# A windowed attention with a two-layer MLP: 128 bytes more behind the tile of queries and keys

## The chip, the cores and the metric

One core of a Trainium2 chip runs the program. The metric is the device time in microseconds (us). "Faster" and "slower" always mean the kernel after the change against the kernel before.

## The reference, cut to what matters

Inputs are `q`, `k`, `v` of shape (8, 8, 576, 64), `moe_w_in` (512, 2048) and `moe_w_out` (2048, 512), all float32. What is computed:

```python
scores = np.matmul(q, k.transpose(0, 1, 3, 2)) / 8
mask_plain = (rel >= 0) & (rel < 32)                         # heads 0 to 3
mask_dil = (rel >= 0) & (rel < 128) & (rel % 4 == 0)         # heads 4 to 7
attn = softmax(where(mask, scores, -1e9))
x = (attn @ v), heads side by side, reshaped to (4608, 512)
h = x @ w_in
g = where(h >= 1, h, where(h <= -1, 0, (h + 1) ** 2 / 4))
out = g @ w_out                                              # (4608, 512)
```

## The kernel before, in words

The two matrix products of the MLP carry nearly all the work. Each of the 4608 tokens' rows belongs to one of nine token tiles of 512 (`t` = 0 to 8), and the 2048 hidden features to sixteen chunks of 128 (`f` = 0 to 15). Operands are split into a high and a low float32r part, and a product is the sum of three matmuls: high by high, high by low, low by high.

- **Layer 1** (`layer1`, the matmuls of line 504): for one (t, f) 12 matmuls (4 blocks of 128 input features, three terms each). The stationary operand is a 128x128 slice of the weight tile `wi`, the moving operand 512 columns of `xh` or `xl`. The result is the PSUM bank `h`.
- **Activation** (lines 514 to 536): VectorE clamps, ScalarE squares, VectorE takes the larger, ScalarE casts the high part `gh`, VectorE subtracts to get the low part `gl`.
- **Layer 2** (`layer2`, line 550): for one (t, f) 12 matmuls (4 blocks of 128 tokens, three terms each). The stationary operand is a 128x128 slice of `gh` or `gl`, the moving operand 512 columns of the weight tile `wo`. The results add up in four PSUM banks `acc` over all f.

I call the 12 matmuls of one layer at one (t, f) a group. There are 9 x 16 groups of each layer. Weight tile `wi0` holds the high and low part of f = 0 and 1, `wi1` of f = 2 and 3, and so on to `wi7` (f = 14 and 15); `wo0` to `wo7` likewise. `weight` (line 488) cuts the slices: one of 128 columns starts a multiple of 512 bytes behind the start of its tile.

The attention runs beside it, on pairs of heads (n = 0 to 31). Queries and keys of a pair, already transposed on the host, come by one DMA into one tile with the tag `qk` (`load_qk`, line 112; queries in columns 0 to 575, keys in columns 576 to 1183), and the values of two pairs into one tile with the tag `v` (`load_v`). In the loop over (t, f) a pair's values are multiplied and the scores of the next pair are made in a *visit* (`visit_step`, line 579; matmuls of line 383 and line 205) between layer 1 and layer 2 of every fourth step; 24 pairs are done so. The stationary slices of `v` follow each other at 256 bytes, the moving slices of `pts` at 384 bytes (line 383).

Order of work. For token tile 0 a list written out by hand (`FIRST`) gives the order on all five engines; it also holds the loads and the splitting of the weights (`raw`, `P`, `B`, `J`, `D`, `E`). The weight blocks are loaded in this order: wi0, wi1, wo0, wi2, wo1, wo3, wi6, wo4, wi3, wo2, wi4, wo7, wi7, wo6, wi5, wo5. For tiles 1 to 8 a loop writes the order of TensorE and of the SP queue (which issues the DMAs): layer 1 of step s, layer 2 of step s - 2, with the attention's pieces in fixed slots; the other engines are ordered by the scheduler. Step s is (t, f) = divmod(s, 16).

Where the tiles lie. A pool puts its tiles one behind the other in a partition, in the order in which their tags are first asked for, so a tile's address follows from the sizes of those ahead of it. In bytes of a partition:

| tiles, in order of address | first and last start | start modulo 256 | modulo 512 |
|---|---|---|---|
| small, pts | 1152, 3712 | 128 | 128 |
| wi6, wo6, wi7, wo7, three xh, three xl | 8320 to 82048 | 128 | 128 |
| two c | 90240, 93568 | 128 | 128, 384 |
| qk (4736 bytes) | 96896 | 128 | 128 |
| v | 101632 | 0 | 256 |
| wi0 to wi5, wo0 to wo5, three gh, three gl, y, m0, m1, mixed | 107776 to 220416 | 0 | 256 |

All sizes behind `qk` are multiples of 2048 bytes, and so are those of the wi, wo, xh and xl ahead of it. The last tile ends at byte 228608.

Of the kernel before, what the change touches and what calls it, by code (L numbers as in the profile page):

```python
# [6 lines left out]
F32 = mybir.dt.float32  # L7
# [7 lines left out]
B, H, S, D = 8, 8, 576, 64  # L15
# [4 lines left out]
KPAD = S + 32  # L20
# [44 lines left out]
def body(ctx, tc, qk, v, mask, mask4, w_in, w_out, out):  # L65
# [4 lines left out]
    pool = ctx.enter_context(tc.tile_pool(name="pool", bufs=1))  # L70
# [41 lines left out]
    def load_qk(n):  # L112
        hd = heads.setdefault(n, {})
        if "qk" not in hd:
            hd["qk"] = pool.tile([128, S + KPAD], F32, tag="qk", name=f"qk{n}")
        hd["q"], hd["k"] = hd["qk"][:, :S], hd["qk"][:, S:]
        nc.sync.dma_start(out=hd["qk"], in_=qk[n])

# [460 lines left out]
    def visit_step(s, n):  # L579
        o, sc = visit(s, n)  # L580
        joint_values(n, o)
        if n + 1 < NP:
            scores(n + 1, at=sc)
        if n + 2 < NP:
            load_qk(n + 2)
        if n + 1 < NP and n % 2:
            load_v(n + 1)
# [37 lines left out]
    def small_step(count):  # L625
        small_constants(int(count), banks_of((4, 5), "small")[1])

    STEPS = {
        "fill": filling_step, "small": small_step,
        "qk": pair(load_qk), "v": lambda n, q=None: load_v(int(n), QUEUES[q]),  # L630
        "raw": lambda _, name, q=None: fetch((name[:2], int(name[2:])), queue=QUEUES[q]),
        "S": lambda n: scores(int(n), BANKS.get("S" + n)),
# [135 lines left out]
```

## Time and profile before

| | us |
|---|---|
| median of 3 runs | 897.12 (896.67 to 897.38) |
| the profiled execution's own time | 897.7 |
| its span, first to last instruction | 895.9 |
| TensorE matmul busy | 885.3 (99%) |
| VectorE busy | 546.4 (61%) |
| ScalarE busy | 305.0 (34%) |
| GpSimd busy | 126.7 (14%) |

The 1.8 us between the profiled time and the span lie around the program's instructions. The profile's engines are PE (TensorE matmul), PEld (TensorE weight load, beside PE), DVE (VectorE), ACT (ScalarE), POOL (GpSimd), SP (the DMA queue). A matmul's record overlaps the next one's (a mean of 394 ns each), so the time of a group is read from where the next group starts, not from these durations.

### The profile page before, as it was taken

The numbers are of one execution on the slowest core, as the hardware profiler recorded it, in microseconds if no ns is written. First come the engines' busy times: TensorE is split into PE (matmuls) and PEld (weight loads), VectorE is DVE, ScalarE is ACT, GpSimd is POOL, SyncE is SP. The second block draws the span as 40 slices with busy tenths as digits, with TensorE's granted clock in tenths as the row PEclk, the third lists the DMA queues.
The fourth block names the chain that finished last, engine by engine and source line by source line (L and its number), as shares of the span: only waits on it lengthen the run. The fifth ranks groups of instructions, "written<-read, shape, count | busy, mean of one in ns | idle before, by whom it ended". The sixth has DMA issues, their size and how long they took to land.

```text
span 895.9 us, 15568 instructions
## 1 busy us (share of the span) xinstructions
PE 885.3 (99%) x6680; PEld 716.7 (80%) x6680; DVE 546.4 (61%) x888; ACT 305.0 (34%) x490; POOL 126.7 (14%) x80
## 2 busy tenths in 40 slices
PE   8899999999999999999999999999999999999998
PEld 7677778888888888888888888888888888888886
DVE  7888876566666666566666666566656543334332
ACT  3797543222323233323323232223322222222222
POOL 2455441111010111111111010111111000000000
PEclk9999999999999999999999999999999999999999
DMA  9971012101210021101210121002110010001001
GB/s 367 401 308 63 29 63 75 64 28 64 75 60 32 4 99 36 64 28 64 75 64 28 64 75 40 35 17 98 41 63 1 1 48 1 1 0 48 1 1 47
DMA packets 17172, 59.77 MB, mean 67 GB/s; under 512 B 1904, under 2 KB 2160, under 8 KB 15056
## 3 DMA queue, kind: packets, MB, share of 16 engines
q1 hardware_dynamic: 17104, 58.79, 17.8%
q8 instruction: 52, 0.85, 0.4%
q14 instruction: 16, 0.13, 0.0%
HBM read 49.34 MB, written 9.44 MB: 66 GB/s over the span
## 4 chain that ended last, share of the span: by engine, by line
PE 95%; DVE 4%; issue 0%; ACT 0%; POOL 0%; POOLq 0%
PE acc L550 44%; PE h L504 43%; PE os L383 3%; PE os L205 2%; PE s L205 1%; PE o L370 1%; DVE m_wo L475 1%; DVE m_wi L475 0%; DVE gl L536 0%; DVE c L273 0%; PE s L184 0%; PE fill L138 0%; PE s L223 0%; PE small L145 0%; DVE wo_first L341 0%
## 5 line engine op out<-in xcount | busy, mean ns | idle before, releaser
L550 PE MATMUL acc<-wo,gh 128*128 128x512 f32 x1152 | 383.7, 394 | 0.0
L504 PE MATMUL h<-xh,wi 128*128 128x512 f32 x1152 | 362.4, 394 | 0.2
L504 PEld LDWEIGHTS h<-xh,wi 128*128 128x128 f32 x1152 | 216.1, 188 | 51.0 <-DVE gl L536 1.0
L550 PEld LDWEIGHTS acc<-wo,gh 128*128 128x128 f32 x1152 | 216.4, 188 | 50.2 <-ACT gh L531 0.4
L550 PE MATMUL acc<-wo,gl 128*128 128x512 f32 x576 | 225.7, 392 | 1.4 <-DVE gl L536 1.4
L504 PE MATMUL h<-xl,wi 128*128 128x512 f32 x576 | 227.0, 394 | 0.0
L520 ACT ACTIVATE y<-y,small 128x512 f32<-128x512 f32 x144 | 104.1, 723 | 318.9 <-DVE y L514 318.9
L514 DVE TENSOR_SCALAR y<-h 128x512 f32<-128x512 f32 x144 | 99.2, 689 | 125.3 <-PE h L504 124.2
L524 DVE TENSOR_TENSOR h<-h,y 128x512 f32<-128x512 f32 x144 | 100.5, 698 | 99.4 <-ACT y L520 99.4
L536 DVE TENSOR_TENSOR gl<-h,gh 128x512 fp32r<-128x512 f32 x144 | 99.3, 690 | 55.1 <-ACT gh L531 53.5
L504 PEld LDWEIGHTS h<-xl,wi 128*128 128x128 f32 x576 | 108.1, 188 | 24.9 <-DVE xl L357 0.3
L550 PEld LDWEIGHTS acc<-wo,gl 128*128 128x128 f32 x576 | 108.3, 188 | 24.6 <-DVE gl L536 1.7
L531 ACT CAST gh<-h 128x512 fp32r<-128x512 f32 x144 | 84.5, 587 | 103.9 <-DVE h L524 101.7
L281 POOL TENSOR_TENSOR c<-c 96x768 f32<-96x768 f32 x28 | 41.2, 1472 | 439.2 <-DVE c L273 438.8
L317 DVE STREAM_TRANSPOSE pts<-c 32x384 f32<-32x384 f32 x168 | 95.3, 567 | 3.0 <-POOL c L303 0.6
L303 POOL TENSOR_TENSOR c<-c 96x768 f32<-96x768 f32 (+1 forms) x30 | 43.5, 1450 | 87.9 <-DVE c L299 87.9
L288 DVE TENSOR_REDUCE c<-c 96x12 f32<-96x768 f32 (+1 forms) x30 | 28.0, 933 | 38.8 <-ACT c L285 38.8
L285 ACT ACTIVATE c<-c 96x768 f32<-96x768 f32 (+1 forms) x30 | 25.0, 834 | 49.0 <-POOL c L281 38.7
L353 ACT CAST xh<-os 128x384 fp32r<-128x384 f32 (+7 forms) x48 | 19.2, 400 | 42.0 <-DVE c L249 21.9
L383 PEld LDWEIGHTS os<-pts,v 128*64 128x64 f32 x576 | 24.6, 137 | 8.8 <-DVE gl L536 6.6
L383 PE MATMUL os<-pts,v 128*64 128x96 f32 x576 | 29.1, 250 | 0.0
L205 PE MATMUL s<-qk 64*32 64x64 f32 x1188 | 27.0, 220 | 0.8 <-issue 0.8
(100 smaller groups left out, 389.9 us busy)
## 6 DMA issues: line engine op xcount, KB each, us to landing
qk<-qk_in SPq DMA_DIRECT2D x29, 592.0 KB, 3.9
v<-v_in SPq DMA_DIRECT2D x29, 384.0 KB, 4.7
raw_wi<-w_in SPq DMA_DIRECT2D x8, 1024.0 KB, 14.4
raw_wo<-w_in SPq DMA_DIRECT2D x8, 1024.0 KB, 15.4
out<-out SPq DMA_DIRECT2D x32, 256.0 KB, 2.0
wi_first<-qk_in SPq DMA_DIRECT2D x2, 592.0 KB, 6.8
out<-outs SPq DMA_DIRECT2D x4, 256.0 KB, 2.0
wo_first<-v_in SPq DMA_DIRECT2D x2, 384.0 KB, 9.3
```

The costliest lines, as they stand in the source:

```text
L205: PE.matmul(out=sps[j][QB * g : QB * g + QB, KW * t : KW * t + KW], lhsT=hd["q"][r, QB * b : QB * b + QB], rhs=hd["k"][r, QB * b : QB * b ...
L281: nc.gpsimd.tensor_tensor(out=c, in0=c, in1=spread(n, 0), op=ALU.subtract)
L303: engine.tensor_tensor(out=c, in0=c, in1=spread(n, 2), op=ALU.mult)
L317: nc.vector.transpose(out=pt[r : r + 32, :, 32 * g : 32 * g + 32], in_=c[32 * g : 32 * g + 32, :, 32 * h : 32 * h + 32],)
L383: PE.matmul(out=at[64 * j : 64 * j + 64, 96 * t : 96 * t + 96], lhsT=hd["v"][:, j, t], rhs=pts[:, j, t], start=True, stop=True,)
L504: PE.matmul(out=hp, lhsT=weight("wi", f, w, slice(128 * c, 128 * c + 128)), rhs=xtile(t)[x][:, c], start=start and (c, w, x) == terms[0], ...
L514: nc.vector.tensor_scalar(out=gs[t, f][0], in0=hps[t, f], scalar1=-1.0, scalar2=1.0, op0=ALU.max, op1=ALU.min)
L520: nc.scalar.activation(out=y, in_=y, func=AF.Square, bias=half_t, scale=0.5)
L524: done.append([nc.vector.tensor_tensor(out=hp, in0=hp, in1=gs[t, f][0], op=ALU.max)])
L531: done[-1].insert(0, nc.scalar.copy(out=g_tile("gh", t, f), in_=hps[t, f]))
L536: nc.vector.tensor_tensor(out=g_tile("gl", t, f), in0=hp, in1=gh.bitcast(F32), op=ALU.subtract)
L550: PE.matmul(out=acc[m], lhsT=g[:, 128 * m : 128 * m + 128], rhs=weight("wo", f, w, slice(0, DM)), start=f == 0 and i == 0, stop=f == NF - ...
```

## The change: what it does

The `qk` tile is asked for with 1216 columns instead of 1184, that is 4864 bytes instead of 4736, and the first 1184 columns are used as before. Nothing else differs: the same instructions with the same shapes, the same DMA of 592 KB per pair. The `qk` tile itself starts where it did. Every tile behind it (v, wi0 to wi5, wo0 to wo5, gh, gl, y, m0, m1) starts 128 bytes later: at 128 modulo 256, or 384 modulo 512.

```diff
@@ load_qk (line 112)
         if "qk" not in hd:
-            hd["qk"] = pool.tile([128, S + KPAD], F32, tag="qk", name=f"qk{n}")
+            hd["qk"] = pool.tile([128, 1216], F32, tag="qk", name=f"qk{n}")[:, :S + KPAD]
         hd["q"], hd["k"] = hd["qk"][:, :S], hd["qk"][:, S:]
```

## Rows read from the trace of the kernel before

**Rows 1.** The page: busy time by engine, and the chain that ended last.

```profile
span 895.9 us, 15568 instructions
PE 885.3 (99%) x6680; PEld 716.7 (80%) x6680; DVE 546.4 (61%) x888; ACT 305.0 (34%) x490; POOL 126.7 (14%) x80
...
PE 95%; DVE 4%; issue 0%; ACT 0%; POOL 0%; POOLq 0%
PE acc L550 44%; PE h L504 43%; PE os L383 3%; PE os L205 2%; PE s L205 1%; PE o L370 1%; DVE m_wo L475 1%; DVE m_wi L475 0%; DVE gl L536 0%; DVE c L273 0%; PE s L184 0%; PE fill L138 0%; PE s L223 0%; PE small L145 0%; DVE wo_first L341 0%
```

**Rows 2.** Busy time by stretch: us, each engine's busy time and count, clock, DMA.

```profile
125.60:321.00 195.40, 195.39 (x1538) 158.77 (x1539) 125.12 (x206) 58.48 (x100) 25.74 (x18) 1.00 0.15 53
321.00:700.00 379.00, 379.00 (x2941) 307.55 (x2942) 240.34 (x397) 113.61 (x193) 44.65 (x31) 1.00 0.14 49
700.00:789.70 89.70, 89.70 (x409) 73.36 (x410) 35.26 (x52) 22.62 (x36) 0.00 (x0) 1.00 0.03 12
```

**Rows 3.** The chain of waits, token tile 8: start us, us, what.

```profile
798.06 2.79 PE h L504 x12
...
803.64 2.78 PE h L504 x12
...
812.01 2.74 PE acc L550 x12
814.75 2.79 PE h L504 x12
817.54 2.73 PE acc L550 x12
...
858.96 2.79 PE h L504 x12
...
864.50 2.73 PE h L504 x12
...
872.69 2.73 PE acc L550 x12
875.42 2.73 PE h L504 x12
878.15 2.80 PE acc L550 x12
880.94 2.76 PE h L504 x12
883.70 8.38 PE acc L550 x36
```

**Rows 4.** The chain of waits where tile 1 passes into tile 2.

```profile
204.53 2.73 PE h L504 x12
207.26 2.73 PE acc L550 x12
...
220.49 2.79 PE acc L550 x12
223.28 2.79 PE h L504 x12
...
237.22 1.14 PE os L383 x24
```

**Rows 5.** Line 383: durations min/median/max ns, and what ended its engine's idle time (us, times).

```profile
L383 PE MATMUL os<-pts,v x576: 246/246/297, 139.8 to 700.9; 128*64 128x96 f32 x192
...
  DVE gl L536: 6.6, 18
```

**Rows 6.** Timeline ahead of one visit: start us, us, what.

```profile
480.04 0.69 DVE L536 TENSOR_TENSOR gl<-h,gh 128x512 fp32r<-128x512 f32 x1
...
480.84 0.28 PEld L383 LDWEIGHTS os<-pts,v 128*64 128x64 f32 x6 [0.37 <-DVE gl L536]
```

**Rows 7.** Token tile 0: busy time by stretch, columns as in rows 2.

```profile
28.00:60.00 32.00, 29.81 (x214) 22.81 (x210) 28.66 (x41) 26.97 (x39) 15.39 (x7) 1.00 0.99 409
60.00:100.00 40.00, 40.00 (x346) 32.26 (x346) 33.84 (x50) 30.05 (x41) 23.49 (x11) 1.00 0.16 52
100.00:125.60 25.60, 25.45 (x262) 19.58 (x260) 22.28 (x31) 15.17 (x23) 10.33 (x6) 1.00 0.24 80
```

**Rows 8.** Token tile 0: two pieces of the chain of waits.

```profile
38.48 3.90 DVE m_wi L475
...
106.78 3.43 DVE m_wo L475
```

**Rows 9.** Weight loads: busy time by stretch, the last two columns DMA share and GB/s.

```profile
38.00:42.90 4.90, 4.90 (x23) 3.95 (x22) 4.90 (x3) 2.61 (x4) 3.29 (x2) 1.00 1.00 419
49.20:56.60 7.40, 7.40 (x47) 5.87 (x46) 7.12 (x11) 6.74 (x8) 2.42 (x1) 1.00 1.01 425
```

**Rows 10.** Timeline of the SP queue: the issues of wi4 and of wo6.

```profile
35.12 0.43 SPq L449 DMA_DIRECT2D raw_wi<-w_in  x1
...
38.04 0.33 SPq L449 DMA_DIRECT2D raw_wo<-w_in  x1
```

**Rows 11.** DMA issues about 35.2 us and about 38.2 us: KB, us to landing.

```profile
raw_wi<-w_in SPq DMA_DIRECT2D x1, 1024.0 KB, 14.1
...
raw_wo<-w_in SPq DMA_DIRECT2D x1, 1024.0 KB, 18.6
```

## The prediction

> **What bounds the kernel now.** I read the page first: the matmuls of TensorE are busy for 99% of the span, and the chain that ended last lies 95% on PE, 44% on line 550 (layer 2) and 43% on line 504 (layer 1) [rows 1]. No other engine is above 61%. Next I asked for busy time by stretch. From 125.6 us, where token tile 1 begins, PE has no idle time worth a name (195.39 of 195.40 us, 379.00 of 379.00), at a granted clock of 1.00, the upper of the two levels, 2.4 GHz [rows 2]. So from there the kernel can get faster only if the matmuls themselves follow each other faster, and anything that lengthens them shows at once.
>
> The change moves addresses and nothing else. So the third question is whether TensorE's pace depends on addresses, and the trace of before holds that experiment: the tiles ahead of `qk` start at 128 modulo 256 bytes, those behind it at 0, and groups of the same 12 matmuls draw their two operands from either side. The chain of waits merges each group into a piece, and PE has no idle time there, so a piece's length is the pace. In token tile 8 the pieces alternate, layer 1 of f, then layer 2 of f - 2. They come in two lengths [rows 3]:
>
> - Layer 1, f = 0 to 11 (twelve pieces, 798.06 to 858.96; weights wi0 to wi5 at 0, moving xh and xl at 128): 2.78 to 2.79 us.
> - Layer 1, f = 12 to 14 (from 864.50 to 875.42; wi6, wi7 at 128, xh and xl at 128): 2.73 us; f = 15, after a layer-2 group of the other kind, 2.76.
> - Layer 2, f = 0 to 11 (812.01 to 872.69; gh and gl at 0, wo0 to wo5 at 0): 2.73 to 2.74 us.
> - Layer 2, f = 12 (878.15): 2.80 us, and f = 13 to 15 together 8.38, or 2.79 each (gh and gl at 0, wo6 and wo7 at 128).
>
> Neither operand's address alone sorts them: moving data at 128 is slow with weights at 0 and fast with weights at 128. What sorts them is whether both operands have the same remainder modulo 256. The same split stands 600 us earlier, with the attention running beside it: layer 1 of f = 13 2.73 us, layer 2 of f = 11 2.73, layer 2 of f = 13 2.79, layer 1 of the next tile's f = 0 2.79 [rows 4]. A difference of 0.06 us per group, or 5 ns per matmul.
>
> **The change, part by part.** After it, `gh`, `gl`, wi0 to wi5 and wo0 to wo5 start at 128 modulo 256, as wi6, wi7, wo6, wo7, xh and xl already do. Every group then has two operands with the same remainder.
>
> *Tiles 1 to 8.* The 34 pieces from 798.06 to the end of the last (883.70 + 8.38 = 892.08) take 94.02 us; at 2.73 each they would take 92.82. Of the 1.20 us over, 0.12 belongs to two layer-2 groups of tile 7 (f = 14 and 15, run in this stretch). That leaves 1.08 us per tile: 16 slow groups at 0.06, and 0.12 in groups that follow a slow one. Eight tiles: 8.6 us. It lies on PE without cover, so it comes off the end. Bounds: 0.05 us for each of the 128 slow groups (6.4), and 1.25 us per tile by the rounding of the pieces (10.0).
>
> *Visits.* The values of line 383 take 1.14 us per visit [rows 4]. Their `v` slices move and `pts` does not; by the slice steps of 256 and 384 bytes the pair of operands takes both remainders before and after, and the 576 matmuls are alike within 246 to 297 ns, with a median at the minimum [rows 5]: no cost. But TensorE arrives earlier, and the first weight load of a visit waits for VectorE, 18 times for line 536 [rows 5]. In the visit shown `gl` ends at 480.73 and the load starts at 480.84 [rows 6]: 0.11 us of slack, where layer 1 ahead of it becomes 0.06 shorter. So most visits keep the gain; I take off 0.3 us for those with less slack, between 0 and 1.4 (24 visits that lose 0.06 each). What is late next there is VectorE's `gl`.
>
> *Token tile 0.* Its 16 slow groups would give 1.0 us. But from 28 to 60 us PE is idle for 2.2 us, VectorE is busy for 28.7 of 32 [rows 7], and single VectorE pieces of 3.9 and 3.4 us stand on the chain [rows 8]. Between 0 and 1.0 I take the middle, 0.5.
>
> *Loads.* Twelve of the sixteen weight blocks now land at 128 instead of 0 modulo 256. wi4 lands at 35.12 + 14.1 = 49.2 us and wo6 at 38.04 + 18.6 = 56.6 [rows 10, 11], so the stretch between carries wo7, wi7 and wo6, which land at 128 already: 425 GB/s, against 419 in a stretch with wo4 and wi3, which land at 0 [rows 9]. No cost is seen; 1.4% of the 30 us that twelve blocks take is 0.4 us, and I keep that on both sides. Work of the other engines covers it; without cover it would be 0.4 us later. The Trainium skill, DMA: Bandwidth & Descriptors, section How a descriptor splits into AXI transactions, says that a descriptor that doesn't start at a multiple of 256 bytes needs an extra transaction; by an estimate from that page, 33 instead of 32 per 8 KB, or 0.9 us over the twelve blocks, the gain would be 0.9 us smaller. The trace does not show it, and the measurement decides.
>
> *The rest.* Stores from m0 and m1, and the DVE, ACT and POOL work on moved tiles, have engines idle for a third of the time or more to cover them [rows 1]. So they are set at zero.
>
> Sum: 8.6 + 0.5 - 0.3 = 8.8 us. The profiled execution took 897.7, with a span of 895.9, and would take 888.9; the median of before is 897.12, 0.6 below that execution, so I forecast 888.3. The forecast's own range is 886.1 (10.0 + 1.0) to 892.4 (6.4 - 1.4 - 0.4 = 4.6, rounded up a little).
>
> **The rivals.** A measurement of this kernel can tell about 0.2%, 1.8 us, from no change.
>
> *Slower: the pattern repeats at 512 bytes, not 256.* Slices of 512 bytes all behave alike, so a period above 512 is excluded, but none of the long matmuls shows an offset of 256. After the change the formerly slow groups have exactly that: weights (wi0 to wi5, or gh and gl) at 384, moving data (xh and xl, or wo6 and wo7) at 128 modulo 512. If 256 is the worst place rather than a good one, these 144 groups grow instead of shrinking. As a price I take the present excess twice (0.12 in place of 0.06): +0.06 x 144 = 8.6 us, or 905.7. It decides as soon as a group at offset 256 takes over 2.79 us. Against it: the visits' matmuls take all four multiples of 128 as offsets modulo 512, and all last alike [rows 5]; but they are short. For it: nothing but the gap in the evidence. A partial conflict at 256 would leave part of the gain.
>
> *No change: it is not the remainder.* The fast and slow pairs are also sorted by whether both operands lie ahead of `qk` or both behind. If the distance or the region in the partition is what counts, 128 bytes change nothing: 897.1. Against it: far-apart tiles on the same side are as fast as near ones (wi6 and the first xh, 33 KB apart; gh and wo5, up to 70 KB apart) [rows 3].
>
> *No change: addresses do not matter at all.* The Trainium skill, SBUF - State Buffer, section Who interferes with whom, gives TensorE two independent read ports, for weights and moving data, and says that it waits for nobody; by that the pairing could not matter and the time would stay at 897.1. The 2.73 and 2.79 us pieces with the same instructions speak against it [rows 3, 4].
>
> **How the numbers follow.** Forecast 0.72; slower by the period 0.14; the two cases of no change 0.10 and 0.04. The predicted time is the forecast's, 888.3. Its own range leaves out nearly 3 in 10, so the range is widened to take in the cases of no change: 886.1 to 897.5. Faster by over 0.2%: 0.72; within 0.2%: 0.14; slower: 0.14.
>
> **What would show it.** In the chain of waits of the changed kernel all groups of token tiles 1 to 8 should take 2.73 us, f = 0 to 11 of layer 1 and f = 12 to 15 of layer 2 among them, and the last layer-2 piece 8.19 instead of 8.38. The first weight load of a visit should wait for line 536 a little more often. Token tile 0 should end about 0.5 us earlier. The prediction is wrong if those groups stay at 2.79 (region, or no address effect), or grow past it (period 512); it is right for the wrong reason if the groups stay and the time goes elsewhere.

## The result, and the profile after

The changed kernel takes 887.19 us (887.08 to 887.29, 4 runs) against 897.25 (896.67 to 897.63, 4 runs): a ratio of 0.9888, interval 0.9871 to 0.9906, or 10.06 us less. Forecast were 888.3, 8.8 us less. The profiled execution took 887.17 us with a span of 885.4, 10.5 less than the span of before.

The page of the changed kernel, to be held against [rows 1]:

```profile
span 885.4 us, 15568 instructions
PE 874.8 (99%) x6680; PEld 715.9 (81%) x6680; DVE 546.3 (62%) x888; ACT 305.1 (34%) x490; POOL 126.8 (14%) x80
...
PE acc L550 44%; PE h L504 43%; PE os L383 3%; PE os L205 1%; PE s L205 1%; DMA wi_first<-mask_in 1%; PE o L370 1%; DVE m_wo L475 1%; DVE m_wi L475 1%; DVE gl L536 0%; DVE wo_first L341 0%; DVE c L273 0%; DVE c L251 0%; DVE xl_first L341 0%; ACT gh L531 0%
```

The counts are those of before. In the two traces the instructions of the engines stand in the same order, but for neighbouring score matmuls and a few weight loads of TensorE and one pair of VectorE instructions that swap places. The other engines' busy times agree with [rows 1] within 0.1 us. TensorE's matmuls alone lost more, 10.5 us, and that is all that the span lost. (Two of the kernels below had one execution that was disturbed, 970 and 4442 us; these are left out of their times.)

The chain of waits of token tile 8, start us, us, what, to be held against [rows 3]; here layer 1 of f = 0 starts at 789.09 and that of f = 15 at 870.69:

```profile
789.09 2.72 PE h L504 x12
791.81 2.72 PE acc L550 x12
...
848.93 2.72 PE h L504 x12
...
854.37 2.72 PE h L504 x12
...
865.25 2.72 PE h L504 x12
867.97 2.72 PE acc L550 x12
870.69 2.72 PE h L504 x12
873.41 8.17 PE acc L550 x36
```

Every group of either layer takes 2.72 us, those between the lines shown too, and the last three together 8.17 instead of 8.38. There are no two lengths any more. One thing is to be seen that was not forecast: layer 1 of f = 12 to 14 (854.37 to 865.25), whose operands wi6, wi7, xh and xl did not move, went from 2.73 to 2.72 too.

Busy time by stretch, with the columns of [rows 2], and the loads, with those of [rows 9]:

```profile
310.00:689.00 379.00, 379.00 (x2960) 311.31 (x2959) 242.43 (x401) 115.70 (x198) 47.13 (x32) 1.00 0.15 53
...
38.00:42.90 4.90, 4.90 (x23) 3.91 (x21) 4.90 (x4) 2.48 (x4) 2.86 (x2) 1.00 1.01 418
49.20:56.60 7.40, 7.40 (x53) 5.96 (x52) 7.14 (x11) 7.05 (x8) 2.43 (x1) 1.00 1.02 423
```

In 379.00 us TensorE starts 2960 matmuls instead of 2941 (the visits do not fall on quite the same places of the two stretches), at the same clock and still without idle time. The loads move 418 and 423 GB/s, against 419 and 425.

### The profile page after: what moved, and what is told of

Read it like the earlier page. It is cut to its first block, busy times and chain, and to the rows that moved or that the text cites. A ratio compares the mean times of both kernels' runs of the same rounds, so it can differ in the third digit from the quotient of the medians.

```text
span 885.4 us, 15568 instructions
## 1 busy us (share of the span) xinstructions
PE 874.8 (99%) x6680; PEld 715.9 (81%) x6680; DVE 546.3 (62%) x888; ACT 305.1 (34%) x490; POOL 126.8 (14%) x80
## 4 chain that ended last, share of the span: by engine, by line
PE 94%; DVE 4%; DMA 1%; ACT 0%; issue 0%; SPq 0%; POOL 0%; POOLq 0%
PE acc L550 44%; PE h L504 43%; PE os L383 3%; PE os L205 1%; PE s L205 1%; DMA wi_first<-mask_in 1%; PE o L370 1%; DVE m_wo L475 1%; DVE m_wi L475 1%; DVE gl L536 0%; DVE wo_first L341 0%; DVE c L273 0%; DVE c L251 0%; DVE xl_first L341 0%; ACT gh L531 0%
## 5 line engine op out<-in xcount | busy, mean ns | idle before, releaser
L504 PE MATMUL h<-xh,wi 128*128 128x512 f32 x1152 | 358.1, 390 | 0.2
L504 PE MATMUL h<-xl,wi 128*128 128x512 f32 x576 | 224.3, 389 | 0.0
```

What stands on the lines that cost most here:

```text
L504: PE.matmul(out=hp, lhsT=weight("wi", f, w, slice(128 * c, 128 * c + 128)), rhs=xtile(t)[x][:, c], start=start and (c, w, x) == terms[0], ...
```

## The experiments

The theory: TensorE's pace depends on the difference between the starts of a matmul's two operands modulo 256 bytes. The rivals are the region in the partition, an operand's own address, and a period of 512. "Offset" is the start of the moving data less that of the weights, modulo 256. Each kernel was run on one chip beside the kernel of before, which took 897.1 to 897.3 us there.

**Move by 384 bytes.** The same remainder modulo 512, not only modulo 256.

```diff
-            hd["qk"] = pool.tile([128, 1216], F32, tag="qk", name=f"qk{n}")[:, :S + KPAD]
+            hd["qk"] = pool.tile([128, 1280], F32, tag="qk", name=f"qk{n}")[:, :S + KPAD]
```

> The tile of queries and keys takes 5120 bytes: everything behind it moves by 384 bytes and starts at 128 modulo 256 and modulo 512, exactly like the tiles ahead of it. Theory A (both operands of a matmul need the same remainder modulo 256, and nothing finer than that matters): all groups of 12 matmuls of tiles 1 to 8 at 2.72 us, 887.2 us as after the change. Rival B (the pattern has a period of 512, and an offset of 256 as after the change is only a good place, not the best): the groups get shorter than 2.72 us, below 886. Rival C (128 bytes are special in another way, an absolute address): above 889.

Measured: 887.03 us, ratio 0.9887 (0.9858 to 0.9915), span 885.4 as after the change. An offset of 256 is as good as one of 0: the period is not 512. That was the rival on the slower side.

**Move by 256 bytes.** The same line with 1248 columns.

> The tile takes 4992 bytes: everything behind it moves by 256 bytes and starts at 0 modulo 512. Theory A: the remainders differ again by 128 from those of xh, xl, wi6, wi7, wo6 and wo7, so layer 1 of f = 0 to 11 and layer 2 of f = 12 to 15 are back at 2.79 us and the time at 897 us. Rival D (any move away from the old place helps, for example because of what lies at the end of the partition): below 890. Rival B (period 512): a third value, apart from 897 by over 2 us.

Measured: 897.09 us, ratio 0.9995 (0.9983 to 1.0006). In the chain of waits of tile 8 the two lengths are back, in their old places (layer 1 of f = 11 and 12, then layer 2 of f = 12):

```profile
858.22 2.79 PE h L504 x12
...
863.76 2.73 PE h L504 x12
...
877.41 2.80 PE acc L550 x12
```

So it is not the size of the tile nor the move as such.

**Move xh and xl too.** Kernel of before, with wo7 longer by 128 bytes:

```diff
     def big(tag, name, dt=F32):
         bufs = 3 if tag in ("xh", "xl") else 1
+        if tag == "wo7":
+            wide = pool.tile([128, 4 * TOK + 32], dt, tag=tag, name=name, bufs=bufs)
+            return wide[:, : 4 * TOK].rearrange("p (a x) -> p a x", a=4)
         return pool.tile([128, 4, TOK], dt, tag=tag, name=name, bufs=bufs)
```

> Kernel of before, but the tile wo7 is 128 bytes longer, so that all tiles behind wo7 move by 128 bytes: xh, xl start at 0 modulo 256, wi0 to wi5, wo0 to wo5, gh and gl at 128, and wi6, wi7, wo6, wo7 stay at 128. Theory A: layer 1 is slow for all 16 f (2.79 us), layer 2 fast for all 16 f (2.72 us); the number of slow groups is 16 per tile as before, so about 897 us, but in other places. Rival E (what counts is whether both tiles lie ahead of qk or both behind it): the groups keep the lengths of before, layer 1 of f = 12 to 15 fast and layer 2 of f = 12 to 15 slow.

Measured: 897.19 us, ratio 1.0004 (0.9993 to 1.0016). The chain of waits of tile 8 (the edit moves line 504 to 507 and 550 to 553), layer 1 of f = 13 to 15 among it:

```profile
869.50 2.79 PE h L507 x12
872.29 2.73 PE acc L553 x12
875.03 2.79 PE h L507 x12
877.82 2.73 PE acc L553 x12
880.55 2.79 PE h L507 x12
883.35 8.19 PE acc L553 x36
```

The time is the same to 0.1 us, and the slow groups have changed places: layer 1 of f = 12 to 15, fast before, takes 2.79, and layer 2 of f = 12 to 15, slow before, takes 2.73 (8.19 for three). wi6, wi7, xh and xl still lie on the same side of `qk`, so the rival of the region falls.

**Move both operands.** Kernel of before, with everything behind the first tile 128 bytes later:

```diff
-    small = const.tile([128, 9 * KW + 64], F32, name="small")
+    small = const.tile([128, 9 * KW + 96], F32, name="small")
```

> Kernel of before, but the first tile (small) is 128 bytes longer, so that every later tile moves by 128 bytes: those ahead of qk start at 0 modulo 256, those behind at 128. Theory A (the difference of the two operands counts): nothing changes, the groups keep their 2.73 and 2.79 us in their places, 897 us. Rival C (an operand's own remainder counts, such as weights at 0 modulo 256 being bad): layer 1 of f = 0 to 11 drops to 2.72 us, or layer 2 of f = 0 to 11 rises, by over 4 us in all.

Measured: 897.32 us, ratio 0.9997 (0.9987 to 1.0008); the chain of waits has the old lengths in the old places (layer 1 of f = 11 and 12, layer 2 of f = 12):

```profile
858.72 2.79 PE h L504 x12
...
864.25 2.73 PE h L504 x12
...
877.90 2.80 PE acc L550 x12
```

Every remainder is another and nothing changed. It is the difference that counts, not an operand's own address.

**Move by 64 bytes.** 1200 columns.

> The tile takes 4800 bytes: everything behind it moves by 64 bytes and starts at 64 modulo 256, the tiles ahead at 128. It shows how fine the pattern is. If only the bit of 128 bytes of the addresses counts (banks of 128 bytes), an offset of 64 overlaps half of the time: slow groups between 2.72 and 2.79 us, 890 to 895 us. If every offset other than 0 modulo 256 is equally bad: 897 us. If only 128 is bad: 887 us.

Measured: 894.98 us, ratio 0.9978 (0.9966 to 0.9989). In the chain of waits of tile 8, layer 1 of f = 1 and 2 stands between the last layer-2 groups of tile 7, all at offset 64, and then the layers alternate between 64 and 0. The last two lines are layer 1 of f = 12 and layer 2 of f = 10:

```profile
798.65 2.75 PE acc L550 x12
801.39 2.75 PE h L504 x12
804.14 2.75 PE acc L550 x12
806.89 2.75 PE h L504 x12
809.63 2.73 PE acc L550 x12
812.37 2.76 PE h L504 x12
815.13 2.77 PE acc L550 x12
...
862.16 2.76 PE h L504 x12
864.93 2.73 PE acc L550 x12
```

Three things are to be seen. Offset 64 by itself costs less than half of what 128 does: 2.75, or 0.03 over 2.72 against 0.07. And layer 2 at 815.13, whose operands both lie at 64, an offset of 0, takes 2.77, more than the groups at offset 64. So a group can pay for its neighbours as well as for its own offset, but not at a fixed price: layer 2 at 809.63, which also has an offset of 0 behind a group at 64, takes 2.73. And layer 1 at 862.16 takes 2.76 although its operands both lie at 128 and those of the layer-2 groups around it both at 64: every offset there is 0, and only the remainder that both operands share changes from group to group.

**Move by 192 bytes.** 1232 columns.

> The tile takes 4928 bytes: everything behind it moves by 192 bytes and starts at 192 modulo 256, so the offset between moving data and weights in the formerly slow groups is -64 instead of the +64 of the move by 64 bytes, where layer 1 of f = 0, 1 took 2.747 us per group against 2.720 at offset 0 and about 2.79 at 128. If the distance from a multiple of 256 counts, in either direction: again 2.75 us for layer 1 of f = 0, 1 and about 895 us in all. If the excess grows with the offset from 0 up to 256: 2.80 us or more, 898 us or more. If it falls from 128 on both sides differently: between 887 and 895.

Measured: 898.76 us, one execution, so no interval. Layer 1 of f = 0 and 1 with a layer-2 group of tile 7 between, all at offset 192, then layer 2 of f = 1 at an offset of 0, and at the end layer 1 of f = 12 and layer 2 of f = 10:

```profile
798.89 2.80 PE h L504 x12
801.69 2.80 PE acc L550 x12
804.49 2.80 PE h L504 x12
...
818.46 2.74 PE acc L550 x12
...
865.52 2.73 PE h L504 x12
868.25 2.76 PE acc L550 x12
```

It is not the distance from a multiple of 256 that counts. By offset a group takes 2.72 us at 0, 2.75 at 64, 2.79 at 128, 2.80 at 192, and 2.72 again at 256.

The last two lines are the groups of the move by 64 bytes that have an offset of 0 on every side; layer 2 now lies at 192 instead of 64, and the two lengths have changed places. So the pair of operands of one and the same matmul is not the whole cause. In both runs the group with 2.76 is the one whose weights lie 64 bytes above the data of the group before it, by their remainders (an offset of 192), and the group with 2.73 the one whose weights lie 64 bytes below (an offset of 64). This would fit a weight load that is held up by the stream that runs while it loads. It is not shown: weights and moving data change their remainder at the same border, and the next run, where theory A1 is this rule, does not bear it out by itself.

**Mix the remainders inside a group.** Kernel of before; `qk` is asked for between xh and xl, the parts of wi0 and wi1 lie 128 bytes apart in their remainders, and the terms of f = 0 to 3 are put in another order:

```diff
+        if n == 3:
+            heads[0]["qk"] = pool.tile([128, S + KPAD], F32, tag="qk", name="qk0")
...
+        if name == "wi" and u < 2:
+            wide = pool.tile([128, 2112], F32R, tag=f"{name}{u}", name=f"{name}{u}")
+            parts = (32, 1088) if u == 0 else (0, 1056)
...
-                layer1(*steps[s])
+                layer1(*steps[s], SWAPPED if steps[s][1] < 4 else ALL)
```

> Kernel of before with the remainders modulo 256 mixed inside a group: the qk tile lies between xh and xl, so xh is at 128 and xl at 0; the high and low parts of wi0 start at 128 and 0, those of wi1 at 0 and 128, all other weights as before. Layer 1 of f = 0 to 3 takes its terms in the order high by high, high by low, low by high. Theory A1 (a weight load collides with the moving data that stream while it loads, those of the matmul before): no load of f = 0, 1 differs from the stream that runs, so about 2.73 us per group; all loads of f = 2, 3 differ, about 2.79; f = 4 to 11 two of three, between. Rival A2 (what counts is the pair of operands of one and the same matmul): f = 0, 1 have two of three pairs that differ, f = 2, 3 one of three, so f = 2, 3 are shorter than f = 0, 1, and both lie between 2.72 and 2.79. Rival A3 (any mixture spoils the pace): all of f = 0 to 11 at 2.77 us or more.

Measured: 894.97 us, ratio 0.9983 (0.9970 to 0.9995). Layer 1 of f = 1 to 4 and 11 in the chain of waits of tile 8 (here line 515):

```profile
800.90 2.76 PE h L515 x12
806.44 2.78 PE h L515 x12
811.98 2.77 PE h L515 x12
817.52 2.75 PE h L515 x12
...
855.92 2.75 PE h L515 x12
```

This run decides nothing between its theories, and all three missed. f = 1 is not at 2.73 (against A1), f = 2 and 3 are longer than f = 1 (against A2), and f = 4 to 11 are under 2.77 (against A3). It says only that mixed remainders cost something of their own. Whether a weight load collides with the stream that runs, or what else makes a matmul wait, stays open.

**The 128 bytes behind v.** Kernel of before:

```diff
-                hd["v"] = pool.tile([128, 1536], F32, tag="v", name=f"v{n}")[:, :768]
+                hd["v"] = pool.tile([128, 1568], F32, tag="v", name=f"v{n}")[:, :768]
...
-            both = pool.tile([128, 1536], F32, tag="v", name=f"v{n}")
+            both = pool.tile([128, 1568], F32, tag="v", name=f"v{n}")[:, :1536]
```

> Kernel of before, but the tile of values (v) is 128 bytes longer instead of qk, so that everything behind v moves by 128 bytes as in the change and v itself stays where it was before, at 0 modulo 256. Theory A with no part for v: 887.2 us, the same as after the change within 0.3 us. Rival F (in the changed kernel the layer-2 group behind a visit got longer, 2.98 us there, because v moved): those 24 groups shorten to the 2.95 of before, and the time falls to about 886 us.

Measured: 886.41 us (886.03 to 886.94), ratio 0.9879 (0.9863 to 0.9896). The same remainders brought about at another tile give the gain of the change. To see whether the 0.8 us were real it ran again, beside the changed kernel on the same chip.

> The changed kernel once more, beside the next one on the same chip: 887.2 us.

> The kernel with the 128 bytes behind v instead of qk once more: if the 0.8 us that it was ahead of the change is real, 886.4 us here and the changed kernel 887.2 on the same chip; if it came from another chip, both the same.

Measured: 886.74 us (885.97 to 887.00) for the changed kernel and 885.97 (885.85 to 886.05) with the bytes behind v; ratios to before 0.9882 (0.9867 to 0.9897) and 0.9875 (0.9860 to 0.9889). It is about 0.8 us again, but the intervals overlap, and so do the times of single executions. First the changed kernel on this chip, two visits with the layer-2 group behind each:

```profile
186.75 1.16 PE os L383 x24
188.81 2.94 PE acc L550 x12
...
210.81 1.16 PE os L383 x24
212.87 2.97 PE acc L550 x12
```

Then the kernel with the bytes behind v, the same two visits:

```profile
186.27 1.14 PE os L383 x24
188.31 2.95 PE acc L550 x12
...
210.33 1.14 PE os L383 x24
212.37 2.95 PE acc L550 x12
```

In the changed kernel's first trace, on another chip, both groups took 2.99; the first of them:

```profile
188.75 2.99 PE acc L550 x12
```

So the length of the group behind a visit differs as much between two executions of one kernel as between the kernels (the granted clock from 125 to 700 us is 0.97 in the first of these three traces and 1.00 in the other two, but groups away from visits take 2.72 in all of them). By the starts of the matmuls the 24 groups behind a visit together take 69.38 and 68.86 us in the two traces of the changed kernel, and 68.57 and 68.65 in those with the bytes behind v. Half of the 0.8 us between the two traces on this chip lies ahead of all that: the first layer-1 matmul starts at 27.72 against 27.31 us. That where `v` lies plays a part in how TensorE settles behind a visit is therefore not shown. Two more kernels asked after it.

**pts at another remainder.** The changed kernel, with `small` and `pts` 128 bytes longer each:

```diff
-    small = const.tile([128, 9 * KW + 64], F32, name="small")
-    pts = const.tile([128, 2, NB // 3, 96], F32, name="pts")
+    small = const.tile([128, 9 * KW + 96], F32, name="small")
+    pts = const.tile([128, 1184], F32, name="pts")[:, :1152].rearrange("p (j t x) -> p j t x", j=2, x=96)
```

> The changed kernel with the tile pts, the moving data of the values' matmuls, at 0 instead of 128 modulo 256, and everything else at the remainders of the changed kernel. Theory G (the group behind a visit settles sooner where pts and v have different remainders, since v at 0 and pts at 128 did in the kernel with the 128 bytes behind v): groups behind a visit 2.85 us by the intervals of their matmuls instead of 2.90, 886.4 us. Rival H (v's own remainder counts, or where v lies against gh and wo): no change, 887.2 us.

Measured: 886.38 to 886.76 us in four executions, ratio 0.9881 (0.9865 to 0.9898); there is no chain of them to read. The changed kernel took 886.74 on that chip: no gain clear of noise, and nothing for theory G.

**qk at another remainder.** Kernel of before:

```diff
-            hd["c"] = pool.tile([128, 832], F32, tag="c", name=f"c{n}", bufs=2)
+            hd["c"] = pool.tile([128, 848], F32, tag="c", name=f"c{n}", bufs=2)
...
-        cc = pool.tile([128, 832], F32, tag="c", name=f"c{n}", bufs=2)[:96]
+        cc = pool.tile([128, 848], F32, tag="c", name=f"c{n}", bufs=2)[:96]
```

> Kernel of before with 64 bytes more in each of the two c tiles: qk starts at 0 instead of 128 modulo 256, v and everything behind it at 128 as in the change. The long groups are as in the change. If the scores' operands (qk, the last matmuls of a visit) set how the group behind a visit settles, those 24 groups change and the time leaves 887.2 us by up to 1 us to either side; if not, 887.2 us.

Measured: 886.49 us (886.27 to 886.97), ratio 0.9881 (0.9866 to 0.9896): 0.25 us below the changed kernel beside it, within its range. The long groups are as in the change, which 64 bytes in each of two other tiles bring about as well. Whether `v` does anything behind a visit is not settled.

## Why the prediction was right, point by point

**The pairing of remainders** was the argument, and it held. It was read out of the kernel of before, where the allocation had put the operands of 128 of the 256 groups of tiles 1 to 8 apart by accident. Moving xh, moving everything, and moving by 256 and 384 bytes all did what the difference modulo 256 says, in the places that it names.

**Tiles 1 to 8** were forecast at 8.6 us, by a floor of 2.73 us per group. That floor was too high: after the change all groups take 2.72. A fast group of before stood beside groups of the other layer whose operands lie at another remainder, and paid for that. Layer 1 of f = 13 shows it, the first line here, between the layer-2 groups of f = 10 and 11: none of its tiles moved, and its own offset and those of both neighbours are 0, but it lies at 128 and they at 0 (chain of waits of before).

```profile
869.96 2.73 PE h L504 x12
872.69 2.73 PE acc L550 x12
```

Tile 8's 34 groups went from 94.02 to 92.49 us (789.09 to 873.41 + 8.17), 1.53 instead of the 1.20 that I counted. From the first layer-1 group of tile 1 (125.61, and 124.59 after) to the end of the last group (892.08, and 881.58) it is 766.47 against 756.99: 9.5 us. So the term was undersized by about 1 us, though the visits gave some back (below).

**Visits.** I took off 0.3 us for visits that wait longer for `gl`. Line 383's idle time by line 536 was 6.6 us before and is 6.3 now, again 18 times, and the records of its matmuls are as long as before (the view of that line, changed kernel):

```profile
L383 PE MATMUL os<-pts,v x576: 246/246/297, 138.5 to 693.4; 128*64 128x96 f32 x192
...
  DVE gl L536: 6.3, 18
```

So the waits that I took off are nothing. The cost that a visit does carry, how the group behind it settles, I had not seen: by the starts of the matmuls the 24 groups behind a visit take 68.81 us before, and 69.38 and 68.86 in the two traces of the changed kernel, so they took back 0.05 to 0.57 us. That the 0.3 lies between is luck.

**Token tile 0** ends 1.02 us earlier (125.61 to 124.59), the upper bound of my 0 to 1.0; I had taken 0.5. But 0.43 of that stands before the first layer-1 matmuls, which start at 27.70 instead of 28.13 us (the chain of waits, changed kernel and before), and has nothing to do with their pace. The 16 groups gave the other 0.6, near what I took; the pieces of VectorE on the chain kept their lengths (3.89 and 3.44 us, against [rows 8]). The 0.43 us are scatter from one execution to the next: in the chains of waits of the other kernels that start is at 27.31 us with the 128 bytes behind v and at 28.17 with the 128 bytes in the two `c` tiles, both with the changed remainders, and at 27.48 in the move by 256 bytes, which took the time of before.

**Loads** cost nothing, as taken: 423 GB/s where the blocks lay at 128 already and 418 where wo4 and wi3 now do. The extra transaction that the Trainium skill names (DMA: Bandwidth & Descriptors, How a descriptor splits into AXI transactions) would by an estimate from that page be 3% of a block; these rows show under 1%. The page tells it of transactions that read, and what moved here is where the blocks are written.

**The sum** came to 8.8 us, measured were 10.06 by the medians. The spans differ by 10.5 because the profiled execution of before lay 0.45 us above its median: 9.5 in tiles 1 to 8, 0.6 in tile 0 and 0.4 ahead of it. The step that was off is the floor of 2.73 us per group; the mechanism was right.

**The rivals.** The period of 512 fell with the move by 384 bytes, which was as fast (887.03 against 887.19 us). [Rows 5], which I held against it, could not speak to it: they give the lengths of records that overlap, and not the distance from one matmul to the next. The region fell with the move of xh and xl. That addresses do not matter fell with the result itself: the Trainium skill (SBUF - State Buffer, Who interferes with whom) has TensorE's two read ports independent and waiting for nobody, and 5 ns in each matmul that come and go with the operands' difference are not that. Whether it is the ports, the memory behind them or the order of loads that makes them wait, no run here shows.

## What to carry to other kernels

Where TensorE has no idle time, merge the chain of waits into groups of equal matmuls and compare the same matmuls on different tiles: two lengths for one instruction are an experiment that the allocator has already made. If the weights' and the moving data's tiles start at different remainders modulo 256 bytes, padding one tile ahead of them costs 128 bytes of each partition and was worth 1.1% here. When the gain of such a step is worked out, the fast groups that border on groups at another remainder are no floor: they gain too.

## What the runs showed of the hardware that was not expected

- The excess of a group of 12 matmuls of 128x128 by 512 grows with the offset between moving data and weights and falls back at 256: 2.72 us at 0, 2.75 at 64, 2.79 at 128, 2.80 at 192 (one execution), 2.72 at 256. It is not symmetric.
- Groups with an offset of 0 pay for their neighbours: 2.73 us where they alternated with groups at offset 128, 2.74 beside 192 and 2.77 beside 64, and up to 2.76 where every offset was 0 and only the shared remainder changed from group to group. Mixing remainders inside groups gave 2.76 where one simple rule of collision promised 2.73.
- The matmuls settle over several matmuls behind an interruption: the group behind a visit took 2.94 to 3.00 us against 2.72, and differed between two executions of the same kernel (2.99 and 2.94 at one visit).
